# Windowed attention followed by an 8-expert mixture: GpSimd's scatters issued in smaller, more frequent turns during attention, and the first half of W2 of expert 0 staged two attention slots before the experts

## The chip, the core and the metric

The program runs on one core of a Trainium2 chip. The core has a matrix engine (TensorE, PE in the profile, with its weight loads shown as PEld), a vector engine (VectorE, DVE), a scalar engine (ScalarE, ACT), GpSimd (POOL) and SyncE (SP, which here only issues DMAs), and 16 DMA engines. The metric is the device time in microseconds of one execution; lower is better. The kernel before was timed three times.

## The reference

Two stages, all in float32. First, causal attention for 8 batches, 8 heads, 576 positions and 64 channels, with two masks: heads 0 to 3 see the last 32 positions, heads 4 to 7 every fourth of the last 128.

```python
rel = pos[:, None] - pos[None, :]
mask_plain = (rel >= 0) & (rel < window)                                   # window 32
mask_dil = (rel >= 0) & (rel < window * dilation) & (rel % dilation == 0)  # dilation 4
scores = np.where(masks[None, :, :, :], scale * q @ k.T, -1e9)
attn = softmax(scores); out = attn @ v
```

The result, as 4608 rows of 512 channels, goes through a mixture of 8 experts. Each row has noisy gate logits, the two largest pick two experts, and their softmax gives two weights:

```python
noisy_logits = x @ w_gate + np.log1p(np.exp(x @ w_noise)) * noise
top2 = np.argpartition(-noisy_logits, 2, axis=1)[:, :2]
h = np.maximum(x[mask] @ w1[e], 0.0)               # 512 -> 1024
out[mask] += top2_w[mask, k, None] * (h @ w2[e])   # 1024 -> 512
```

## The kernel before, in words

**Attention** is cut into 24 pieces (four groups of two batches, each with three pieces of dilated and three of plain heads), and runs as a software pipeline of 26 steps, each of two slots (`kb` = 2i and 2i+1). In step i the core computes the scores of piece i (`qk`, L354: mask and 24 x 4 score matmuls into the PSUM tile `s`, then on VectorE the row maximum `mx` and the shifted scores `a`), transposes the exponentials of piece i-1 (`ptr`, ScalarE copies them out as `pt`), multiplies them with the values (`pv`, output tile `x`, L426), and for piece i-2 stores `x` to DRAM (`xs`), transposes it and multiplies it with the gate matrices (`gate_mm`). `s` has one PSUM buffer and `a` one SBUF buffer; `x` has three.

**Routing** runs between these. `gate(t0, n)` (L513) is a generator for n tiles of 128 rows: some 45 small VectorE and ScalarE instructions and a few matmuls that find the two experts of each row and the slot `si` of each in a table in DRAM. Then, for each tile, one indirect DMA of GpSimd (`fill_slots`, L628) scatters the 128 entries of the first choice into the table; that of the second choice goes on `backlog`. There are 72 of these scatters. When enough of the table is there, SyncE reads it back (`ixf<-tab`), and GpSimd gathers the rows of `xs` for the first expert by 20 indirect DMAs (L770, two for each tile of 128 rows); `xsplit` transposes and splits a gathered tile.

**The order is written out by hand.** Every engine runs its instructions in the order in which the Python emits them. `micro(n)` advances the generators by n instructions (2n at rate 2). `new_slot(scatters)` is called at the end of each slot and grants GpSimd that many turns until the next grant, flushing leftovers from `backlog`; before the grant of a slot with turns is used, `pace` emits a one-element copy (`spacer<-x`) on GpSimd that reads the newest `x`, so that the turns wait for that output; the further turns of a grant are preceded by a `memset` of the spacer, which waits for nothing. Before, even slots grant 4 turns and odd slots none, and a turn of a gather takes both gathers of a tile.

**Experts.** Each expert has three blocks of rows. `up` (L814) multiplies a block with W1 in 8 column tiles `f`, three PSUM buffers in rotation, and ScalarE and VectorE turn each into `hh` and `hl`; `down` multiplies with W2 and scatters rows to the output with accumulation (L845). Work beside the matmuls is put on a schedule, `plan(t, f)`, whose clock `now` advances by the columns of the matmuls emitted (`tick`). In the first expert `some()` grants one turn every microsecond of that clock, and `some_of_slots` emits six backlog scatters in a row behind the newest `hh`. Weights pass through two staging buffers `ws` shared by W1 and W2.

Of the kernel before, what the change touches and what calls it, by code (L numbers as in the profile page):

```python
# [46 lines left out]
def attention_moe_kernel(ctx, tc, qt, kp, kd, vpl, vdl, w_gate, w_noise, noise, w1, w2, out, CAPS=(1216, 1216, 1216, 1184, 1184, 1152, 1152, 1152), SPLITS=(0, 384, 896)):  # L47
# [243 lines left out]

    fresh, backlog = [True], []

    def new_slot(scatters, speed=1):
        if scatters:
            while room[0] > 0 and backlog and not experts[0]:
                pool_turn()
                backlog.pop(0)()
            room[0], fresh[0] = scatters, True
        rate[0] = speed  # L300
        held.clear()

    def pace(yes=True):

        if yes and late["x"] is not None:
            gpsimd.tensor_copy(spacer, late["x"])  # L306
        else:
            gpsimd.memset(spacer, 0.0)

    def pool_turn():  # L310


        pace(fresh[0] and not experts[0])
        fresh[0] = False
        room[0] -= 1
# [38 lines left out]
    def qk(k):  # L354
# [22 lines left out]
        vector.tensor_tensor(a.rearrange("p y e c -> p e y c"), s[:, 0:6], mx.unsqueeze(3).to_broadcast([128, 6, 2, 64]), op=OP.subtract)  # L377
        SB[k] = a

    def expo(k):  # L380
# [379 lines left out]
    X = {}  # L760
    GT = {}

    def gather(e, t):
        r0, rn = TLS[e][t] if e != "o" else (0, 128)
        g = gp_.tile([128, 4, 128], F32, name="g")
        if e == 0:

            rows = 2304 * (next((i for i in range(U - 1) if r0 + rn <= SPLITS[i]), U - 1) + 1)
            for c in range(2):
                gpsimd.indirect_dma_start(  # L770
                    out=g[0:rn, 2 * c:2 * c + 2].rearrange("p c d -> p (c d)"), out_offset=None, in_=xs[0:rows],
                    in_offset=bass.IndirectOffsetOnAxis(ap=IX[0][0][0:rn, t, c:c + 1], axis=0))
            GT[e, t] = g
            return
        if e != "o":
            pace()
        for j in range(rn // 32):
            gpsimd.indirect_dma_start(out=g[:, j], out_offset=None, in_=xq,  # L778
                                      in_offset=bass.IndirectOffsetOnAxis(
                                          ap=IX[e][1][:, r0 // 32 + j:r0 // 32 + j + 1], axis=0))  # L780
        GT[e, t] = g
# [161 lines left out]
    def first_blocks(bi):  # L943
        for t in range(BLS[0][bi][0], BLS[0][bi][1]):
            yield from wait_turn()
            room[0] -= 1
            gather(0, t)
            if bi == 0:
# [3 lines left out]
    def split_first(bi, t):  # L952
        xsplit(0, bi, t)()
        done[bi] += 1

# [7 lines left out]

    for t0, n, kb in ((0, 9, 17), (9, 9, 29), (18, 6, 39), (24, 3, 41), (27, 6, 51)):
        at(kb, lambda t0=t0, n=n: gens.append(gate(t0, n)))
# [29 lines left out]
    for kc in range(4):  # L995
        a, b = ((-3, 2), (-2, 3), (4, 6), (5, 7))[kc]
        at(L0 + SL_W1 + a, lambda kc=kc: stage_w1(0, kc))
        at(L0 + SL_W1 + b, lambda kc=kc: late.__setitem__(("w", kc), split_w1(kc)))
        at(L0 + SL_W1 + b + 1, lambda kc=kc: late.pop(("w", kc))())
    def fillers(kb):  # L1000
        slot[0] = kb + 1
        for f in fill.pop(kb, []):
            f()
        new_slot((4, 0)[kb % 2], 1 if kb < 28 else 2)

# [72 lines left out]
    for e in range(E):  # L1078
# [12 lines left out]
        t = start if first else at_[0, 1]  # L1091
        plan(t - 6, lambda e=e: (stage_w2(EID[e], 0), stage_w2(EID[e], 1)))
        wo, ws = US_W2 if first else (0.5, 3.0)
# [4 lines left out]
        if first:  # L1098
# [22 lines left out]

            plan(start + 2.5, some_of_slots)
            plan(start + 20, lambda: gens.append(rest_of_slots()))
# [18 lines left out]
        for dn, bi, x, *ab in order:  # L1142
            if dn:
                down(x, bi, *ab)
            else:
                while e == 0 and done[bi] < BLS[0][bi][1] - BLS[0][bi][0]:
                    some()
                    tick(1200)
                up((e, bi), X.pop((e, bi)), BLS[e][bi][3], tail(e, bi))
# [84 lines left out]
```

## Time and profile before

| | |
|---|---|
| device time, median of 3 | 1091.08 us (1090.73 to 1094.09) |
| span of the profiled execution | 1086.8 us; what lies around it, against the median, is 4.3 us |
| PE / PEld busy | 1011.7 us (93%) / 855.7 us (79%) |
| DVE / ACT / POOL busy | 465.7 / 319.4 / 534.5 us |
| HBM read / written | 92.11 / 39.54 MB |
| first score matmul, first `up` matmul, first `down` matmul | 9.56, 227.24, 256.58 us |

The page gives no other time for the profiled execution than its span, so sums below are made against the span and carried to the median by the 4.3 us. A row of a timeline reads: start, duration, engine, line, operation, output<-input, shape, how many were merged, and in brackets how long the engine had been idle before and what ended that. A row of a table by windows reads: stretch, its length, then for each engine busy time and number of instructions, the granted PE clock (1.00 is full speed), the share of time the 16 DMA engines were busy, and GB/s. "remote" and "issue" stand for idle time for whose end the profile has no instruction of another engine to show.

### The profile page before, as it was taken

How to read it: one execution, taken by the hardware profiler on the slowest of the kernel's cores; microseconds unless marked ns; L12 is line 12 of the kernel's file. 1: busy time of each engine (PE TensorE's matmuls, PEld its weight loads, DVE VectorE, ACT ScalarE, POOL GpSimd, SP SyncE). 2: the span in 40 equal slices, each digit the busy share in tenths (PEclk: the TensorE clock that was granted, in tenths of full speed). 3: DMA queues.
4: the chain of work that ended last, by engine and by line, in shares of the span. 5: the costliest groups of instructions: out<-in, count | busy, mean ns of one | idle time of the engine just before them, and what ended most of it. 6: DMA issues, size and time to landing. Idle time of an engine off the chain costs nothing. (4 is left out here: it accounts for less than half of the span.)

```text
span 1086.8 us, 18768 instructions
## 1 busy us (share of the span) xinstructions
PE 1011.7 (93%) x7274; PEld 855.7 (79%) x7275; DVE 465.7 (43%) x1060; ACT 319.4 (29%) x609; POOL 534.5 (49%) x727
## 2 busy tenths in 40 slices
PE   6896877778989999999999999999999999999996
PEld 4774655567878989988997889788978888888885
DVE  7673635635225444344434352435353434343221
ACT  6673534622113322222223131312131222222110
POOL 7004243455776655755644564466455645553112
PEclk9998887878999999999999999999999999999999
DMA  8898687455255243533533352426242623453123
GB/s 280 313 315 278 194 283 257 151 164 186 43 96 129 54 109 85 109 84 86 91 85 85 86 131 50 102 64 135 38 112 52 137 39 108 75 119 72 24 28 45
DMA packets 79214, 132.95 MB, mean 122 GB/s; under 512 B 31648, under 2 KB 41296, under 8 KB 77840
## 3 DMA queue, kind: packets, MB, share of 16 engines
q1 hardware_dynamic: 56768, 92.56, 27.6%
q0 software_dynamic: 22352, 39.15, 19.6%
q8 instruction: 58, 0.95, 0.4%
q14 instruction: 36, 0.29, 0.1%
HBM read 92.11 MB, written 39.54 MB: 121 GB/s over the span
## 5 line engine op out<-in xcount | busy, mean ns | idle before, releaser
L826 PE MATMUL up<-x,w1h 128*128 128x512 f32 (+4 forms) x1536 | 396.7, 344 | 10.9 <-issue 8.2
L778 POOL DMA_INDIRECT g<-xs,ixi x258 | 269.7, 1045 | 84.0 <-issue 78.6
L826 PEld LDWEIGHTS up<-x,w1h 128*128 128x128 f32 x1536 | 273.1, 189 | 37.2 <-issue 8.7
L826 PE MATMUL up<-x,w1l 128*128 128x384 f32 (+4 forms) x768 | 263.4, 343 | 0.0
L868 PE MATMUL dn<-w2h,hh 128*128 128x512 f32 x576 | 225.5, 392 | 0.0
L868 PE MATMUL dn<-w2l,hh 128*128 128x512 f32 x576 | 224.7, 390 | 0.0
L868 PE MATMUL dn<-w2h,hl 128*128 128x512 f32 x576 | 224.6, 390 | 0.0
L832 DVE SCALAR_TENSOR_TENSOR hl<-up,hh 128x384 fp32r<-128x384 f32 (+2 forms) x192 | 106.7, 557 | 249.1 <-ACT hh L830 187.0
L830 ACT ACTIVATE hh<-up 128x384 fp32r<-128x384 f32 (+4 forms) x192 | 94.6, 498 | 298.7 <-PE up L826 248.7
L845 POOL DMA_INDIRECT out_rows<-y,ixs x67 | 107.3, 1602 | 141.4 <-DVE y L877 119.0
L826 PEld LDWEIGHTS up<-x,w1l 128*128 128x128 f32 x768 | 145.4, 189 | 11.8
L877 DVE TENSOR_SCALAR y<-dn,ixs 128x512 f32<-128x512 f32 x63 | 47.3, 751 | 188.2 <-PE dn L868 163.5
L868 PEld LDWEIGHTS dn<-w2h,hl 128*128 128x128 f32 x576 | 108.4, 188 | 22.7
L868 PEld LDWEIGHTS dn<-w2h,hh 128*128 128x128 f32 x576 | 108.5, 188 | 22.0
L868 PEld LDWEIGHTS dn<-w2l,hh 128*128 128x128 f32 x576 | 108.5, 188 | 21.8
L797 ACT CAST x<-xr 128x512 fp32r<-128x512 f32 x67 | 40.5, 605 | 216.0 <-DVE xr L795 175.8
L306 POOL COPY spacer<-hh 1x1 f32<-1x1 f32 x72 | 26.4, 366 | 131.9 <-ACT hh L830 131.6
L628 POOL DMA_INDIRECT tab<-en,si x72 | 71.8, 998 | 36.1 <-issue 16.2
L798 DVE TENSOR_TENSOR x<-xr,x 128x512 fp32r<-128x512 f32 x67 | 44.7, 667 | 17.9 <-ACT x L797 12.4
L371 PE MATMUL s<-kt,qt 128*32 128x128 f32 x1152 | 41.2, 288 | 9.9 <-DMA qt<-in_qt 5.4
L371 PEld LDWEIGHTS s<-kt,qt 128*32 128x32 f32 x1152 | 32.5, 115 | 20.3 <-issue 19.6
L708 DVE TENSOR_TENSOR w1l<-ws,w1h 128x1024 fp32r<-128x1024 f32 x32 | 38.8, 1218 | 20.8 <-ACT w1h L706 10.9
(186 smaller groups left out, 867.2 us busy)
## 6 DMA issues: line engine op xcount, KB each, us to landing
ws<-in_moe_w SPq DMA_DIRECT2D x36, 512.0 KB
ws<-in_moe_w SPq DMA_DIRECT2D x112, 128.0 KB
out_rows<-zero SPq DMA_DIRECT2D x38, 256.0 KB
vd<-in_vdl SPq DMA_DIRECT2D x24, 390.0 KB
vp<-in_vpl SPq DMA_DIRECT2D x16, 585.0 KB
qt<-in_qt SPq DMA_DIRECT2D x14, 576.0 KB
xs<-x SPq DMA_DIRECT2D x24, 256.0 KB
kt<-in_kd SPq DMA_DIRECT2D x16, 320.0 KB
```

Source lines behind the costliest of these rows:

```text
L371: tensor.matmul(s[32 * qd:32 * qd + 32, e], lhsT=QV[ty][:, b, x, 32 * ub:32 * ub + 32], rhs=KV[ty][:, :, b, x, 32 * ub:32 * ub + 64], star ...
L628: ins = gpsimd.indirect_dma_start(out=tab, out_offset=bass.IndirectOffsetOnAxis(ap=si[:, kq, t:t + 1], axis=0), in_=en[:, kq, t], in_offse ...
L708: return lambda: vector.tensor_tensor(b, s, a.bitcast(F32), op=OP.subtract)
L778: gpsimd.indirect_dma_start(out=g[:, j], out_offset=None, in_=xq, in_offset=bass.IndirectOffsetOnAxis(ap=IX[e][1][:, r0 // 32 + j:r0 // 32 ...
L797: scalar.copy(xh[:, :, o:o + rn], xr[:, :, 0:rn])
L798: return lambda: vector.tensor_tensor(xl[:, :, o:o + rn], xr[:, :, 0:rn], xh[:, :, o:o + rn].bitcast(F32), op=OP.subtract)
L826: tensor.matmul(p[:, 0:n], lhsT=a[:, 128 * f:128 * f + 128], rhs=b[:, kc, 0:n], start=(i == 0), stop=(i == 11))
L830: scalar.activation(hh[:, f, 0:n], p[:, 0:n], AF.Relu)
L832: vector.scalar_tensor_tensor(hl[:, f, 0:m], p[:, 0:m], 0.0, hh[:, f, 0:m].bitcast(F32), op0=OP.max, op1=OP.subtract)
L845: ins = gpsimd.indirect_dma_start(out=out, out_offset=bass.IndirectOffsetOnAxis(ap=sc[0:rn, t, 1:2], axis=0), in_=y[0:rn], in_offset=None, ...
L868: tensor.matmul(p[0:rn], lhsT=a[:, f, o:o + rn], rhs=b[:, f % 2], start=(i == 0), stop=(i == 23))
L877: vector.tensor_scalar(y[0:rn], p[0:rn], wsc, None, op0=OP.mult)
```

## The change

1. Slots grant 1 turn (even slots) and 2 turns (odd slots) up to slot 49, and 4 from slot 50, instead of 4 and 0. `qk` now records the shifted scores `a` as the newest tile, so the turn of an even slot waits for `a` of piece i, and the two of the odd slot for `x` of piece i-1. The tile waited for is fixed when the slot is granted (`mark`).
2. A turn takes one gather of a tile and not both; a tile is split only when both are out.
3. The first gating call of 9 tiles at slot 17 becomes one of 6 tiles at slot 15 and one of 3 at slot 17, and generators run at rate 2 from slot 16 instead of slot 28.
4. The first two quarters of W2 of expert 0 are staged in slots 49 and 50, and no longer at the first tick of the experts.
5. `some_of_slots` is planned at 10.5 instead of 2.5 us of the first expert's clock. The loop that waits for the first expert's rows no longer advances that clock.

```diff
     def new_slot(scatters, speed=1):
         if scatters:
...
-            room[0], fresh[0] = scatters, True
+            room[0], fresh[0], mark[0] = scatters, True, late["x"]
...
-    def pace(yes=True):
-
-        if yes and late["x"] is not None:
-            gpsimd.tensor_copy(spacer, late["x"])
+    def pace(yes=True, at=None):
+
+        at = late["x"] if at is None else at
+        if yes and at is not None:
+            gpsimd.tensor_copy(spacer, at)
         else:
             gpsimd.memset(spacer, 0.0)
 
     def pool_turn():
-        pace(fresh[0] and not experts[0])
+        pace(fresh[0] and not experts[0], mark[0])
...
         SB[k] = a
+        late["x"] = a[0:1, 0, 0, 0:1]
...
     def first_blocks(bi):
         for t in range(BLS[0][bi][0], BLS[0][bi][1]):
-            yield from wait_turn()
-            room[0] -= 1
-            gather(0, t)
+            for c in range(2):
+                yield from wait_turn()
+                gather(0, t, c)
...
-    for t0, n, kb in ((0, 9, 17), (9, 9, 29), (18, 6, 39), (24, 3, 41), (27, 6, 51)):
+    for t0, n, kb in ((0, 6, 15), (6, 3, 17), (9, 9, 29), (18, 6, 39), (24, 3, 41), (27, 6, 51)):
...
+    at(NK + 1, lambda: stage_w2(0, 0))
+    at(NK + 2, lambda: stage_w2(0, 1))
+
     def fillers(kb):
...
-        new_slot((4, 0)[kb % 2], 1 if kb < 28 else 2)
+        new_slot((1, 2)[kb % 2] if kb < NK + 2 else 4, 1 if kb < 16 else 2)
...
-        plan(t - 6, lambda e=e: (stage_w2(EID[e], 0), stage_w2(EID[e], 1)))
+        if not first:
+            plan(t - 6, lambda e=e: (stage_w2(EID[e], 0), stage_w2(EID[e], 1)))
...
-            plan(start + 2.5, some_of_slots)
+            plan(start + 10.5, some_of_slots)
...
                 while e == 0 and done[bi] < BLS[0][bi][1] - BLS[0][bi][0]:
                     some()
-                    tick(1200)
+                    for t in range(*BLS[0][bi][0:2]):
+                        split_first(bi, t)
```

The first place is GpSimd's order where its scatters begin, in the kernel before and then in the changed one. `tab` is the table, `en` the entries, `x` and `a` are the tiles waited for.

```order
L306 COPY spacer_172<-x_1512 1x1
L628 DMA tab_58<-en0_1452,si0_1520 37376x4
L308 MEMSET spacer_172 1x1
L628 DMA tab_58<-en0_1452,si0_1520 37376x4
L308 MEMSET spacer_172 1x1
L628 DMA tab_58<-en0_1452,si0_1520 37376x4
```

```order
L307 COPY spacer_172<-a_1366 1x1
L630 DMA tab_58<-en0_1337,si0_1406 37376x4
L307 COPY spacer_172<-x_1433 1x1
L630 DMA tab_58<-en0_1337,si0_1406 37376x4
L309 MEMSET spacer_172 1x1
L630 DMA tab_58<-en0_1337,si0_1406 37376x4
L307 COPY spacer_172<-a_1501 1x1
L630 DMA tab_58<-en0_1337,si0_1406 37376x4
```

Before, four scatters follow one wait for `x`; now one follows a wait for `a`, two a wait for the next `x`, and so on in every step, 13 times in a row (steps 11 to 23), with six gathers among these turns.

The second place is GpSimd's order in the first `up` of expert 0, before and then changed. `g<-xs` are gathers of a later block, `hh` is the tile of the `up` that the copy waits for (tile f = 0 before, f = 4 now).

```order
L770 DMA g<-xs,ixf 128x256 x2
L306 COPY spacer<-hh 1x1
L628 DMA tab<-en_2181,si_2280 37376x4
L308 MEMSET spacer 1x1
L628 DMA tab<-en_2877,si_2956 37376x4
```

```order
L773 DMA g<-xs,ixf 128x256
L307 COPY spacer<-hh 1x1
L630 DMA tab<-en_2230,si_2329 37376x4
L309 MEMSET spacer 1x1
L630 DMA tab<-en_2230,si_2329 37376x4
```

The order of the rows is the same (eight gathers stand ahead, six backlog scatters follow the copy); what the copy waits for comes four tiles later. In all, 44 scatters and 14 gathers stood ahead of this copy before; now 40 scatters and 14 gathers.

The third place is SyncE's DMA order at the end of attention, before and then changed. `ws` is the staging of W2, `xs<-x` the store of an attention output, `ixf<-tab` the table read that the gathers of the second block wait for.

```order
L988 DMA out_rows<-zero 128x512 x3
L439 DMA xs<-x 256x1x256
L441 DMA xs<-x 64x1x256 x2
L743 DMA ixf<-tab 128x4x4
L988 DMA out_rows<-zero 128x512
L712 DMA ws_3351<-in_moe_w 128x2x512
L712 DMA ws_3353<-in_moe_w 128x2x512
```

```order
L714 DMA ws_3288<-in_moe_w 128x2x512
L992 DMA out_rows<-zero 128x512
L714 DMA ws_3304<-in_moe_w 128x2x512
L441 DMA xs<-x 256x1x256
L443 DMA xs<-x 64x1x256 x2
L992 DMA out_rows<-zero 128x512 x3
L745 DMA ixf<-tab 128x4x4
```

Both W2 loads now stand ahead of the last store of `x` and of the table read; before, they stood behind both.

More of the change, by code (lines that the diff above doesn't have):

```diff
@@ L290, in attention_moe_kernel @@
     room, held, rate = [0], set(), [1]
-    fresh, backlog = [True], []
+    fresh, backlog, mark = [True], [], [None]
     def new_slot(scatters, speed=1):
@@ L760, in attention_moe_kernel, with gather @@
     X = {}
-    GT = {}
-    def gather(e, t):
+    GT, GOT = {}, {}
+    def gather(e, t, c=None):
         r0, rn = TLS[e][t] if e != "o" else (0, 128)
-        g = gp_.tile([128, 4, 128], F32, name="g")
[L766 to L774, printed above, removed]
+        if e == 0:
+            GOT[t] = c == 1
+            if c == 0:
+                GT[e, t] = gp_.tile([128, 4, 128], F32, name="g")
+            rows = 2304 * (next((i for i in range(U - 1) if r0 + rn <= SPLITS[i]), U - 1) + 1)
+            gpsimd.indirect_dma_start(
+                out=GT[e, t][0:rn, 2 * c:2 * c + 2].rearrange("p c d -> p (c d)"), out_offset=None, in_=xs[0:rows],
+                in_offset=bass.IndirectOffsetOnAxis(ap=IX[0][0][0:rn, t, c:c + 1], axis=0))
+            return
+        g = gp_.tile([128, 4, 128], F32, name="g")
         if e != "o":
@@ L952, in split_first @@
     def split_first(bi, t):
-        xsplit(0, bi, t)()
-        done[bi] += 1
+        if GOT.get(t) and (0, t) in GT:
+            xsplit(0, bi, t)()
+            done[bi] += 1
     def x_block(bi):
```

## The prediction

> **What bounds the kernel now.** I read the page first, then tables by windows, then timelines of GpSimd's bursts.
>
> ```profile
> span 1086.8 us, 18768 instructions
> PE 1011.7 (93%) x7274; PEld 855.7 (79%) x7275; DVE 465.7 (43%) x1060; ACT 319.4 (29%) x609; POOL 534.5 (49%) x727
> PEclk9998887878999999999999999999999999999999
> ```
>
> TensorE is the bound of the whole, but its clock row drops below 9 from the fourth slice to the tenth, that is up to about 270 us. The chain of waits ends in one piece at the end and says nothing on this. So I cut the span by stage:
>
> ```profile
> 53.29:77.52 24.23, 23.31 (x527) 19.05 (x521) 18.17 (x73) 17.62 (x46) 0.43 (x1) 1.00 0.93 318
> 83.44:197.62 114.18, 85.22 (x1428) 63.28 (x1426) 54.17 (x209) 49.50 (x123) 40.69 (x73) 0.82 0.75 242
> 197.62:227.24 29.62, 19.76 (x250) 14.47 (x249) 14.28 (x45) 14.61 (x35) 14.42 (x25) 0.79 0.45 137
> 227.24:256.58 29.34, 21.64 (x109) 20.86 (x108) 15.80 (x80) 7.62 (x16) 14.69 (x25) 0.75 0.63 204
> 256.58:274.98 18.40, 18.40 (x94) 15.17 (x92) 8.61 (x30) 3.17 (x6) 14.72 (x26) 1.00 0.50 154
> 256.58:1078.00 821.42, 814.60 (x4049) 701.44 (x4047) 321.10 (x534) 190.71 (x321) 442.70 (x558) 1.00 0.40 85
> ```
>
> The first stretch is four attention steps without scatters: 6.06 us each, PE busy throughout. The second is eleven steps (12 to 22): 10.4 us each. Then come the tail of attention (step 23 to the first `up`), the first `up`, the first three `down` tiles, and all from there on. From 256.58 PE is busy 814.6 of 821.4 us, though GpSimd is as dense in the fifth stretch (14.7 of 18.4 us) as in the bad ones. So GpSimd's DMAs cost TensorE nothing beside `down`, whose matmuls need few answers from other engines; whatever the change can win lies before 256.58.
>
> Which steps are slow? The scatters (L628) alone, step by step (length, busy and count, clock, DMA share, GB/s):
>
> ```profile
> 77.52:83.44 5.92, 0.00 (x0) 1.00 0.96 311
> 83.44:100.97 17.53, 7.91 (x8) 0.74 0.93 310
> 110.93:116.93 6.00, 0.00 (x0) 1.00 0.65 202
> 116.93:128.56 11.63, 3.83 (x4) 0.75 0.73 229
> 128.56:135.34 6.78, 1.95 (x2) 0.93 0.42 73
> 140.71:155.37 14.66, 7.70 (x8) 0.82 0.97 322
> 155.37:167.83 12.46, 3.84 (x4) 0.67 0.81 261
> 173.84:190.87 17.03, 1.97 (x2) 0.70 0.61 211
> ```
>
> Steps with none take 5.9 to 6.0 us, four scatters add 5.6 and 6.5 us, eight add 11.5 and 8.7, two add 0.8. (The last row has six gathers as well, so eight DMAs, and 11 us.) Gathers and scatters in the eleven steps are 32 and 6:
>
> ```profile
> 83.44:197.62 114.18, 31.05 (x32) 0.82 0.75 242
> 83.44:197.62 114.18, 5.79 (x6) 0.82 0.75 242
> ```
>
> so the excess, 114.18 - 11 x 6.0 = 48.2 us, is 1.27 us for each DMA of GpSimd, nearly its whole time in a burst. How a burst of four does it:
>
> ```profile
> 117.37 0.17 POOL L306 COPY spacer<-x 1x1 f32<-1x1 f32 x1 [11.25 <-DVE x L426]
> 118.05 0.97 POOL L628 DMA_INDIRECT tab<-en,si  x1 [0.51 <-issue]
> 121.85 0.95 POOL L628 DMA_INDIRECT tab<-en,si  x1 [0.23 <-issue]
> 123.97 0.96 DVE L376 TENSOR_REDUCE mx<-s 128x12 f32<-128x768 f32 x1 [6.01 <-remote]
> 124.08 0.86 ACT L397 COPY pt<-pp 128x512 f32<-128x512 f32 x2 [4.49 <-remote]
> 124.72 1.52 PE L414 MATMUL o<-vd,pt 128*32 128x130 f32 x20 [4.26 <-ACT pt L397]
> ```
>
> VectorE and ScalarE stand idle for 6.0 and 4.5 us, and both go on 1.2 us after the last scatter ends (122.80), with the profile naming no engine they waited for; TensorE then lacks `pt`. A burst of two at the same place:
>
> ```profile
> 130.39 0.18 POOL L306 COPY spacer<-x 1x1 f32<-1x1 f32 x1 [7.59 <-DVE x L426]
> 131.08 0.99 POOL L628 DMA_INDIRECT tab<-en,si  x1 [0.51 <-issue]
> 132.37 0.96 POOL L628 DMA_INDIRECT tab<-en,si  x1 [0.21 <-issue]
> 132.97 1.59 PE L414 MATMUL o<-vp,pt 128*32 128x130 f32 x44 [0.62 <-ACT pt L397]
> ```
>
> Here the same matmuls lose 0.62 us.
>
> **The change part by part.** *Attention turns.* Before, a grant is four DMAs behind one wait; now it is one behind `a` and two behind `x`. `a` needs VectorE to have answered TensorE (scores to `mx` to `a`) before the next DMA is issued, so no run is longer than two unless the answers have passed between. Steps 12 to 22 get 11 x 3 = 33 DMAs for 38, and step 11 gets three. The price of a pair is shown once, 0.78 us (6.78 against 6.00), 0.39 for each DMA; that of a single one behind `a` no row shows. Bounds for a step of three: nothing, since one DMA of 0.96 us fits beside ScalarE's exponential; or 3 x 1.27 = 3.8 us, as in bursts. I take the pair's row, the nearest, for all three: 1.17 us. The eleven steps then take 66.0 + 12.9 = 78.9 us and step 11 adds 1.2. A second bound is the DMA engines: the stretch moved 242 GB/s x 114.18 us = 27.6 MB, and at the 318 GB/s of the clean steps that is 87 us. Part of it is zeros for the output and W1, which no attention step waits for, so I take the middle of 78.9 and 87: 83. **Gain 114.2 - 83 - 1.2 = 30 us** (48 if spaced DMAs are free; 48.2 - 12 x 3.8 = 2.6 if each costs what it does in a burst).
>
> *Tail.* Its PE work is 19.76 us at a clock of 0.79, 15.6 us at full speed; the rest of 29.62 is stalls and low clock with 12 scatters. Now nine stand there, five of them spaced and four in a row: 15.6 + 5 x 0.39 + 4 x 1.27 = 22.6. **Gain 7 us** (0 to 14).
>
> *First `up`.* Matmul work is 21.64 us at 0.75, 16.2 at full speed. It loses its largest piece here:
>
> ```profile
> 236.95 0.95 POOL L770 DMA_INDIRECT g<-xs,ixf  x1 [0.30 <-issue]
> 237.90 0.18 POOL L306 COPY spacer<-hh 1x1 f32<-1x1 f32 x1
> 244.67 0.96 POOL L628 DMA_INDIRECT tab<-en,si  x1 [0.22 <-issue]
> 246.61 0.49 ACT L830 ACTIVATE hh<-up 128x384 fp32r<-128x384 f32 x1 [8.21 <-remote]
> 247.75 0.69 PE L826 MATMUL up<-x,w1h 128*128 128x384 f32 x1 [7.69 <-issue]
> ```
>
> Eight gathers run into six scatters, the copy between them finds its `hh` long done, ScalarE answers only when all are through, and with three PSUM buffers full TensorE waits 7.69 us. Now the copy waits for tile 4, so ScalarE must have answered five tiles before the scatters start; what is left, three tiles of `up` at 16.2 / 8 = 2.0 us and fifteen matmuls of a `down` tile at 18.40 / 72 = 0.26, together 9.9 us, covers six scatters and the 1.2 us behind them (6 x 1.27 + 1.2 = 8.8). The gathers are as dense as before, so I leave 2 us of wait and most of the low clock: 23 us. **Gain 6.5 us** (0 to 13).
>
> *W2's first half, earlier.*
>
> ```profile
> 226.31 0.96 SPq L712 DMA_DIRECT2D ws<-in_moe_w  x2
> 231.98 1.04 ACT L719 CAST w2h<-ws 128x1024 fp32r<-128x1024 f32 x1
> ```
>
> Before, it was there without a wait, 5.7 us after its issue, because `up` was slow. It is worth nothing by itself; it keeps ScalarE from standing at that cast when `up` is faster. On SyncE's queue two loads move past the last store of `x` and the table read, each waiting for a staging buffer that VectorE's W1 split frees; the gathers behind get up to 2 us later, ahead of a block that is wanted 15 us on.
>
> *Gating in two calls.* The order has 29 more VectorE rows. At no more than
>
> ```profile
> L614 DVE TENSOR_TENSOR oh<-oh,y 128x144 f32<-128x144 f32 (+2 forms) x6 | 1.5, 249 | 0.0
> ```
>
> 0.25 us each, 7 us go into steps 8 to 11, where VectorE is idle 6.1 of 24.2 us, and twice as many per place. I take 1 us of loss, up to 6 if the order puts them before `mx`.
>
> *A new wait.* `a` has one buffer, and GpSimd now reads it: VectorE's next `a` stands behind that copy, behind it the scores' only PSUM tile, and so TensorE. GpSimd is held up by
>
> ```profile
> POOL tab L628 <- DVE si L625: 15.8, 3, 10.6
> POOL g L770 <- DMA ixf<-tab: 6.2, 1, 6.2
> ```
>
> A step leaves it 6.0 - (2.94 + 1.65) = 1.4 us to spare (a pair with its copy 2.94 from the rows at 130.39, a single 1.65), so the 6.2 us wait for the table can reach TensorE with some 2 us. Loss 2 us.
>
> Sum: 30 + 7 + 6.5 - 1 - 2 = 40.5 us off the span of 1086.8, so 1046.3; with the 4.3 us between span and median, **1050.5 us**. Everything after the first `down` is taken as it is.
>
> **The rivals.** (A) *Half of it*: each spaced DMA costs about 0.9 us, or the loads of keys and values become the bound at 87 us with stalls on top. For it: clean steps already have a DMA share of 0.93 to 0.96. Against: the step from 77.52 has 0.96 and takes 5.92. Attention then wins 48.2 - 12 x 2.7 = 16 us, tail and `up` 6: 1091 - 22 + 3 = 1072.
>
> (B) *The bursts are not the cause.* Slow steps would be those whose loads are late (shares 0.93 and 0.97 in two of them); regrouping changes nothing: 1091 + 3 = 1094 with the losses, or 1091 if they are hidden. Against: steps at 0.61 and 0.73 stall as much. The page "SBUF — State Buffer" of the Trainium skill, section "Who interferes with whom", has GpSimd contend with VectorE alone, for one shared port pair, and says that PE and ACT never wait on anyone. By that rule ScalarE's 4.49 us would not be GpSimd's doing, and this rival would hold. The trace does not agree: ScalarE stood until the scatters were over.
>
> (C) *Slower*: the price goes by the DMA, and GpSimd enters the chain of every step through the single `a`. The step from 155.37 pays 6.46 / 4 = 1.6 us a scatter. At that, twelve steps of three cost 58 us against 48.2, tail and `up` stay as they are, and gating and the table wait add 3: 1091 + 10 + 3 = 1104. It decides once a DMA costs over 48.2 / 36 = 1.34 us. Against: the pair's 0.39.
>
> **How the numbers follow.** Forecast 0.62, A 0.20, B 0.07, C 0.11. The forecast alone spans 1033 (spaced DMAs free and `up` nearly clean: 48 + 8 + 5 - 3) to 1064 (0.7 us a DMA, 48 - 25, tail and `up` 7, less 3); the range for 8 in 10 reaches on through A, to 1080. A difference of 0.3%, 3.3 us, is what a measurement of this kernel can tell from none. Faster by more than that: the forecast, A, and a little of B, 0.83; within it: most of B, 0.05; slower: C and some of B, 0.12.
>
> **What would show it.** Right: attention steps from 11 on last 6 to 7.5 us each with a granted clock near 1.00; the "remote" waits of `mx` and `pt` are under 2 us; step 23 starts near 169 us and the first `up` near 191; no wait of 7.69 us in the first `up`; the part behind the first `down` keeps its 821 us. A step of 9 us or more with clean pairs, or waits of `mx` for a key or query load, would prove A; VectorE's `a` waiting for the copy of GpSimd would prove C. The sum is wrong if the stall goes by the number of DMAs and not by their runs, or if the stalls before `down` reappear as waits of `up` for the gathered rows.

## The result, and the profile after

The changed kernel took 1071.63 us at the median of four runs (1067.71 to 1075.80), the kernel before 1090.90 (1086.58 to 1094.09): a ratio of 0.983, interval 0.980 to 0.987. It is 19.3 us faster, where 40.6 was forecast. The profiled execution has these lines (span; busy time of the engines; granted clock in forty slices):

```profile
span 1066.0 us, 18824 instructions
PE 1001.5 (94%) x7275; PEld 844.3 (79%) x7276; DVE 468.1 (44%) x1088; ACT 319.8 (30%) x612; POOL 537.6 (50%) x737
PEclk9999998989899999999999999999999999999998
```

The clock row is back at 8 or more throughout. Windows of the changed kernel, cut at the same places of the program as the forecast's (step 11; steps 12 to 22; the tail; the first `up`; the first three `down` tiles; the second `up`; the second `down`; all the rest). Columns: window and length, then busy time and count of TensorE's matmuls, its weight loads, VectorE, ScalarE and GpSimd, then clock, DMA share, GB/s:

```profile
76.49:85.36 8.87, 5.84 (x131) 4.74 (x129) 4.78 (x21) 4.56 (x13) 3.52 (x6) 1.00 0.94 291
85.36:177.12 91.76, 74.55 (x1428) 56.02 (x1426) 54.27 (x213) 49.67 (x124) 34.72 (x61) 0.95 0.86 289
177.12:200.19 23.07, 17.84 (x249) 13.45 (x249) 14.34 (x44) 14.52 (x34) 13.63 (x22) 0.84 0.73 223
200.19:217.34 17.15, 17.15 (x111) 16.84 (x109) 11.78 (x63) 6.41 (x14) 9.59 (x18) 1.00 0.74 210
217.34:247.18 29.84, 23.42 (x94) 15.84 (x91) 13.35 (x54) 4.26 (x7) 21.56 (x38) 0.89 0.43 142
247.18:269.93 22.75, 22.75 (x102) 18.30 (x100) 5.59 (x8) 4.18 (x7) 14.97 (x29) 1.00 0.20 37
269.93:297.29 27.36, 21.06 (x83) 16.40 (x81) 3.81 (x6) 2.05 (x4) 20.53 (x34) 0.81 0.44 79
297.29:1066.00 768.71, 754.27 (x3777) 652.88 (x3775) 302.25 (x483) 181.61 (x304) 398.48 (x486) 1.00 0.39 83
```

The last three stages of the kernel before, which the forecast had not cut apart:

```profile
274.98:297.73 22.75, 22.75 (x102) 18.30 (x100) 5.88 (x15) 3.58 (x6) 15.79 (x26) 1.00 0.23 42
297.73:320.05 22.32, 19.59 (x84) 15.08 (x83) 4.41 (x7) 2.42 (x5) 16.41 (x26) 0.92 0.54 96
320.05:1086.80 766.75, 753.85 (x3777) 652.89 (x3775) 302.20 (x483) 181.53 (x304) 397.33 (x484) 1.00 0.39 83
```

Stage by stage, before less after: the start of step 11 comes 1.0 us earlier; step 11 loses 2.9; steps 12 to 22 gain 22.4 (114.18 to 91.76); the tail 6.6; the first `up` 12.2. The first `down` therefore starts 39.2 us earlier, at 217.34 for 256.58, and 40.5 was forecast. Then the three first `down` tiles lose 11.4 us (18.40 to 29.84), the second `down` 5.0, the rest 2.0: 18.5 us are given back where nothing was to change, and 20.8 us of the span are left.

What does the loss look like? TensorE in the second `down` (start, duration, instruction, idle time before it and what ended it), and GpSimd's DMAs there, the first and the last of 21 that follow each other with no pause of a microsecond:

```profile
278.54 0.21 PE L795 MATMUL xrp<-ident,g 64*128 64x64 f32 x1 [0.33 <-issue]
280.64 0.26 PE L795 MATMUL xrp<-ident,g 64*128 64x64 f32 x1 [1.89 <-issue]
282.77 0.26 PE L795 MATMUL xrp<-ident,g 64*128 64x64 f32 x1 [1.86 <-issue]
283.47 0.36 PE L795 MATMUL xrp<-ident,g 64*128 64x64 f32 x1 [0.44 <-issue]
285.08 0.78 PE L871 MATMUL dn<-w2h,hh 128*128 128x512 f32 x1 [1.25 <-issue]
```

```profile
254.83 0.98 POOL L630 DMA_INDIRECT tab<-en,si  x1 [4.94 <-issue]
...
281.09 1.61 POOL L848 DMA_INDIRECT out_rows<-y,ixf  x1 [0.22 <-issue]
```

Four transposes of one tile, which wait for no engine and no transfer ("issue"), start 2.10, 2.13 and 0.70 us apart: multiples of 0.70. From 277.3 to 285.2 nearly every instruction that TensorE starts, weight loads too, is 0.7 us or twice that behind the one before. It ends 2.4 us after the last DMA of the run. The same spacing fills 217.6 to 225.0, beside 14 DMAs from 208.29 on. Behind each series the granted clock is low for some microseconds more; over the two `down` windows it is 0.89 and 0.81. Until the slow starts begin, TensorE runs at full speed beside the same run of DMAs:

```profile
208.29:217.59 9.30, 9.30 (x63) 8.98 (x62) 6.19 (x27) 3.02 (x6) 7.77 (x14) 1.00 0.87 266
254.83:277.28 22.45, 22.45 (x101) 18.02 (x101) 4.84 (x7) 4.17 (x7) 18.78 (x35) 1.00 0.24 43
```

125 starts (63 matmuls and 62 weight loads) in the one, 202 in the other. From here comes the theory that the runs were to test, **S**: during an unbroken run of GpSimd's indirect DMAs each engine has a stock of starts; when it is used up, the engine starts one instruction per 0.7 us until the run is broken. Starts so spaced are called slow starts below. Its rivals: **V**, each GpSimd DMA beside `down` costs a share, however spaced; **L**, the tiles wait for late data.

**Two conditions.** The runs of this study fell into two conditions, those that ran together always into the same one: "held", where the kernel before takes 1090 to 1092 us (as in the result above; mean granted clock 0.956 to 0.973), and "free", where it takes 1027 to 1030 us (0.981 to 0.991). One chip showed both with the same program, and what sets the condition is not known. Each time below stands beside that of the kernel before in the same condition.

### The profile page after: what moved, and what is told of

Same layout as the page of the kernel before. It is cut to its first block, busy times and chain, and to the rows that moved or that the text cites. A ratio compares the mean times of both kernels' runs of the same rounds, so it can differ in the third digit from the quotient of the medians.

```text
span 1066.0 us, 18824 instructions
## 1 busy us (share of the span) xinstructions
PE 1001.5 (94%) x7275; PEld 844.3 (79%) x7276; DVE 468.1 (44%) x1088; ACT 319.8 (30%) x612; POOL 537.6 (50%) x737
## 5 line engine op out<-in xcount | busy, mean ns | idle before, releaser
L800 ACT CAST x<-xr 128x512 fp32r<-128x512 f32 x67 | 40.5, 604 | 216.6 <-DVE xr L798 173.3
L710 DVE TENSOR_TENSOR w1l<-ws,w1h 128x1024 fp32r<-128x1024 f32 x32 | 38.8, 1217 | 21.1 <-issue 11.3
L708 ACT CAST w1h<-ws 128x1024 fp32r<-128x1024 f32 x32 | 33.1, 1049 | 45.1 <-DMA ws<-in_moe_w 45.0
L798 DVE STREAM_TRANSPOSE xr<-g 128x512 f32<-128x512 f32 x67 | 45.7, 682 | 1.7 <-DMA g<-xs,ixi 1.7
```

Source lines behind the costliest of these rows:

```text
L710: return lambda: vector.tensor_tensor(b, s, a.bitcast(F32), op=OP.subtract)
L798: vector.transpose(xr[:, :, 0:rn].rearrange("p c (g t) -> p g c t", t=32), g[:, 0:n].rearrange("p g (c d) -> p g c d", d=32))
L800: scalar.copy(xh[:, :, o:o + rn], xr[:, :, 0:rn])
```

## The experiments

**Breaks in GpSimd's runs.** The edit adds ten small writes of GpSimd to its own spacer ahead of the six scatters behind the gathers, and ten in the middle of the later run:

```diff
+    def idle(n):
+        for _ in range(n):
+            gpsimd.memset(spacer, 0.0)
...
                 while backlog:
+                    if n == 8:
+                        idle(10)
                     pace(n % 4 == 0)
...
             def some_of_slots():
+                idle(10)
                 for i in range(min(6, len(backlog))):
                     pace(i == 0)
```

> The changed kernel with GpSimd idling for some 3 us (ten small writes to its spacer) at two places of the expert phase: ahead of the six table scatters that follow the eight gathers, and once in the middle of the later run of scatters and gathers. Nothing else moves. Theory S (a stock of instructions: TensorE starts some 60 to 200 instructions at full speed after GpSimd begins an unbroken run of indirect DMAs, then one each 0.7 us until the run is broken): the stalls of the first three down tiles (11.4 us) and of the second down (5.0 us) go for the most part, 1054 to 1062 us. Theory V (each GpSimd DMA beside down costs a share, however spaced): 1071 to 1078, since the same DMAs are only later. Theory L (the tiles wait for late data: gathered rows, W2's second half): 1072 to 1080, since the rows come later still.

> The kernel of the first experiment again (GpSimd idles some 3 us ahead of the six table scatters and once in the later run), for a chip with the stalls. Theory S (stock of instructions, used up in an unbroken run): from the first down to the third up 68 to 74 us instead of the changed kernel's 80; the first gather for expert 1 comes some 4 us later, which leaves 1058 to 1066. Theory V (each DMA beside down costs a share however spaced): 80 us and more, 1071 to 1078. Theory L (late data): 82 us and more, 1073 to 1080. On a chip without the stalls: 1037 to 1042, as measured.

> The kernel with two breaks of some 3 us in GpSimd's runs behind attention, once more, for a chip with the stalls. Theory S (stock of instructions, used up in an unbroken run): from the first down to the third up 68 to 74 us instead of the changed kernel's 80, 1058 to 1066. Theory V (each DMA beside down costs a share however spaced): 80 us and more, 1071 to 1078. Theory L (late data): 82 us and more, 1073 to 1080. On a chip without the stalls: 1037 to 1043, as measured twice.

Free: 1039.71 against 1027.72 (ratio 1.0125, 1.0106 to 1.0145) and 1042.22 against 1028.81 (1.012). Held, on the same chip as the second: 1068.89 against 1090.14 (0.980, 0.975 to 0.986). The writes were shorter than planned, 1.4 us, so that DMAs stand 1.7 to 2.3 us apart at a break. In the held run, the first three `down` tiles, the second `up` and the second `down`, and then the stretch from the first break to the first slow start:

```profile
226.57:256.84 30.27, 22.26 (x93) 16.89 (x91) 10.87 (x45) 3.78 (x6) 21.39 (x39) 0.83 0.32 94
256.84:279.58 22.74, 22.74 (x102) 18.30 (x100) 5.76 (x10) 4.18 (x7) 18.71 (x43) 1.00 0.23 42
279.58:297.15 17.57, 17.57 (x84) 14.24 (x82) 3.81 (x6) 2.14 (x4) 10.87 (x20) 1.00 0.51 93
```

```profile
224.43:240.94 16.51, 16.51 (x87) 13.77 (x86) 9.32 (x34) 3.47 (x7) 13.86 (x25) 1.00 0.57 208
```

The second `down` is clean: 17.57 us, TensorE busy in all of it, with nine DMAs beside it (the 27.36 us of the changed kernel have 17). That is against V. On L this run says little: the last gather for that `down` comes 2.7 us later than in the changed kernel (273.65 for 270.90), but the `down` itself begins 9.7 us later. Against L stand the four transposes of one tile above, for which the profile shows no wait for data. The first tiles lost as much as ever, but elsewhere: no slow start behind the break until 173 further starts, at 240.9, in a run that was now 20 DMAs long; then the spacing of 0.7 us until 253. S placed the stall right. From the first `down` to the third `up` it is 70.6 us, within the 68 to 74 expected. The total was missed because in this trace the first `down` came at 226.57, 9.2 us later than in the changed kernel's: 5.3 us of that were lost before the first `up` began, ahead of any break, and 4.0 us in it.

**Three breaks.** None of the runs behind attention longer than some 13 DMAs:

```diff
     def pace(yes=True, at=None):
+        if experts[0]:
+            paced[0] += 1
+            if paced[0] in (9, 19, 36):
+                for _ in range(10):
+                    gpsimd.memset(spacer, 0.0)
```

> The changed kernel with three breaks (ten small writes, 1.4 to 1.6 us) in GpSimd's runs behind attention: behind the eight gathers, ten DMAs later, and in the middle of the later run, so that none is longer than some 13 DMAs. Theory S: no stall of one instruction per 0.7 us is left before the third up; from the first down to the third up 58 to 65 us instead of 80. GpSimd's first gather for expert 1 comes at 290 to 294 us (5 later), and with 768 us behind it that now sets the end: 1058 to 1066 against 1072. Theory V (each DMA costs a share): 80 us and 1072 to 1080. Where there are no stalls: 1038 to 1045.

> The changed kernel with three breaks in GpSimd's runs behind attention, once more. Where there are stalls, theory S: from the first down to the third up 58 to 65 us instead of 80, GpSimd's first gather for expert 1 at 290 to 294 us, and 1058 to 1066 against 1072; theory V: 80 us, 1072 to 1080. Where there are none: 1039 to 1046, as measured.

Free: 1042.50 against 1028.40 (1.0146, 1.009 to 1.020). Held: 1069.11 (1066.94 to 1069.90) against 1090.24, 0.980 (0.978 to 0.981); that is not told apart from the changed kernel's 1071.63. The same three stages and the third `up`, then two waits of TensorE:

```profile
221.29:240.24 18.95, 18.66 (x93) 15.17 (x91) 11.51 (x45) 4.14 (x7) 15.40 (x40) 1.00 0.51 189
240.24:266.68 26.44, 23.18 (x102) 18.21 (x100) 6.53 (x11) 4.67 (x8) 16.84 (x31) 1.00 0.22 32
266.68:288.83 22.15, 19.54 (x82) 15.42 (x82) 3.31 (x5) 1.54 (x3) 16.30 (x37) 0.92 0.16 26
288.83:310.33 21.50, 16.32 (x97) 16.08 (x96) 5.74 (x16) 3.54 (x8) 15.51 (x23) 0.84 0.56 111
```

```profile
266.48 0.44 PE L802 MATMUL xrp<-ident,g 128*128 128x128 f32 x2 [3.26 <-DMA g<-xs,ixf]
301.21 0.87 PE L836 MATMUL up<-x,w1h 128*128 128x320 f32 x2 [5.18 <-ACT hh L840]
```

No slow start is left in these stages, and the first three tiles take 18.95 us instead of 29.84: here S holds. From the first `down` to the third `up` it is 67.5 us instead of 80.0, a little above the 58 to 65 expected. But the time hardly moves. In the place of the slow starts stand waits for GpSimd's products: rows gathered late (3.26), and a ScalarE that stands at the first rows for expert 1 while `up` wants its `hh` (5.18). Where the 12.4 us went shows beside the third `up` and the stage behind it in the changed kernel, and that stage with three breaks:

```profile
297.29:313.45 16.16, 14.55 (x97) 14.08 (x96) 6.91 (x19) 4.07 (x9) 10.51 (x13) 1.00 0.24 54
313.45:333.48 20.03, 20.03 (x90) 16.10 (x89) 11.91 (x16) 6.48 (x9) 15.02 (x18) 1.00 0.66 163
```

```profile
310.33:332.92 22.59, 20.85 (x90) 15.94 (x89) 12.05 (x19) 6.63 (x9) 16.18 (x18) 1.00 0.53 119
```

The first `down` had come 4.0 us later (221.29), the third `up` takes 5.3 us more and the next stage 2.6; the remaining 2.7 us are lost behind that.

S does not hold for every run. In the changed kernel, held, 24 DMAs (gathers for expert 1 and output scatters) follow each other from 315.60 to 350.37 us with at most 0.35 us between two, and TensorE makes 353 starts beside them, busy throughout:

```profile
315.60:350.37 34.77, 34.77 (x177) 31.17 (x176) 17.41 (x25) 9.58 (x16) 28.35 (x32) 1.00 0.55 127
```

So neither an unbroken run nor a number of starts is enough by itself; what differs there was not tested.

GpSimd's first gather for expert 1, in the changed kernel and with three breaks:

```profile
286.68 1.05 POOL L781 DMA_INDIRECT g<-xs,ixi  x1 [0.16 <-POOL spacer L307]
```

```profile
292.18 1.05 POOL L788 DMA_INDIRECT g<-xs,ixi  x1 [0.16 <-POOL spacer L314]
```

**Does GpSimd's chain set the end?** Behind that gather, 767 to 784 us pass until the end in all the traces:

| kernel | condition | that gather at, us | from it to the end of the span |
|---|---|---|---|
| before | held | 306.6 | 780.2 |
| changed | held | 286.7 | 779.4 |
| changed, two breaks / three breaks | held | 291.2 / 292.2 | 775.9 / 776.0 |
| before | free | 257.9 | 770.1 |
| changed | free | 269.0 | 767.9 |
| changed, turns undone | free | 261.1 | 768.1 |
| changed, three turns in every half-step | free | 252.3 | 775.2 |
| changed, without scatters beside `down` | free | 248.4 | 781.1 |

It is never under 767. In the free runs whose gather comes at 257.9 us or later, it is 767 to 771, which fits an end set by GpSimd; where the gather is early, or TensorE stalls, it is longer. That GpSimd sets the end is read from this floor and was not tested by itself. The changed kernel in the held condition is 12 us above the floor, so that there TensorE's path would set the end. With three breaks the gather comes 5.5 us later (2.4 us of it were there when the first `up` began), which would leave about half of the 12 to win; but that run too ends 9 us above the floor, with the losses behind the second `down` named above. No version tried here is faster than the kernel before in both conditions.

**Three turns in every half-step**, all behind `x`, to get the scatters done before the first `up` (the lines that made the single turn wait for `a` are taken out as well):

```diff
-            room[0], fresh[0], mark[0] = scatters, True, late["x"]
+            room[0], fresh[0] = scatters, True
...
-        pace(fresh[0] and not experts[0], mark[0])
+        pace(fresh[0] and not experts[0])
...
-        late["x"] = a[0:1, 0, 0, 0:1]
...
-        new_slot((1, 2)[kb % 2] if kb < NK + 2 else 4, 1 if kb < 16 else 2)
+        new_slot(3 if kb < NK + 2 else 4, 1 if kb < 16 else 2)
```

> The changed kernel with three turns in every half-step, all behind the outputs x, so that most table scatters are through before the first up. Theory G (on a chip without the stalls of 0.7 us an instruction, the end is set by GpSimd: the time from the first gather for expert 1 to the end was 767 to 771 us in seven traces, however early the first down came): some ten scatters fewer behind attention put that gather at 245 to 250 us, 1014 to 1022, below the kernel before's 1028. If TensorE's path set the end there: 1026 to 1032. On a chip with the stalls: runs of six in every step, 1095 to 1120.

> The kernel with three turns in every half-step, all behind x, once more, for a chip without the stalls. Theory G (there the end follows GpSimd: 767 to 771 us from its first gather for expert 1): that gather at 245 to 250 us, 1014 to 1022, below the kernel before's 1028. If TensorE's path set the end: 1026 to 1032. On a chip with the stalls: 1091 to 1097, as measured.

> Three turns in every half-step, all behind x. Where there are no stalls, theory G (the end follows GpSimd, 767 to 771 us from its first gather for expert 1): that gather at 245 to 250 us, 1014 to 1022, below the kernel before's 1028; if TensorE's path set the end, 1026 to 1032. Where there are stalls: 1089 to 1097, as measured twice.

Held: 1094.69 against 1091.70 (1.003, 1.001 to 1.006) and 1091.73 against 1090.14 (1.001): the gain of the change is gone, with steps of up to 16 us. Free: 1028.01 against 1028.40 (1.000). GpSimd's gather did come early, at 252.3, but attention lost 10 us in step 22, so TensorE's path set the end. The 1014 to 1022 were missed.

**The kernels themselves in the free condition.**

> The changed kernel itself, once more. The chip of the first four experiments ran the kernel before in 1027.7 us instead of 1091, and no engine there was held to one instruction per 0.7 us beside GpSimd's DMAs. On a chip without these stalls there is nothing to space: steps 12 to 22 take 66 to 68 us with the change as without it, first down some 198 us, and the time is that of the kernel before within 0.5% (1025 to 1033). On a chip that has them: 1066 to 1076 against 1086 to 1094.

> The kernel before itself, for its trace on this chip. Without the stalls: four scatters in a row leave an attention step at 6.0 to 6.5 us (1.3 to 1.7 us in all for the eleven steps, against 48.2 us in the trace that the forecast was made from), and the wait of 7.69 us in the first up is gone; 1025 to 1031. With the stalls: 1086 to 1094 and steps of 11 to 17 us.

1040.17 for the change against 1027.38 (1.0125, 1.009 to 1.016): here the change is *slower*, by 12.8 us, where I had expected no difference. The kernel before, run as an experiment, took 1029.60 (1.002). Steps 12 to 22 of the kernel before, and its first three `down` tiles:

```profile
86.05:158.05 72.00, 66.71 (x1429) 52.85 (x1426) 53.96 (x209) 49.41 (x123) 33.99 (x63) 1.00 1.00 334
206.30:225.18 18.88, 18.69 (x93) 15.17 (x92) 11.39 (x42) 3.67 (x6) 14.85 (x27) 1.00 0.62 192
```

The eleven steps, with bursts of four as ever, take 72.0 us instead of 114.18, 6.0 above eleven times 6.0 (1.3 to 1.7 had been expected), at a clock of 1.00: there is next to nothing to win by spacing. The wait of 7.69 us in the first `up` is gone. What the change costs there, in the changed kernel's trace:

```profile
157.69 1.01 POOL L773 DMA_INDIRECT g<-xs,ixf  x1 [15.37 <-DMA xs<-x]
...
159.99 0.18 POOL L307 COPY spacer<-a 1x1 f32<-1x1 f32 x1
160.20 0.96 DVE L378 TENSOR_TENSOR a<-s,mx 128x768 f32<-128x768 f32 x1 [9.01 <-POOL spacer L307]
...
161.21 0.80 PE L361 MATMUL s<-mask,identb 128*128 128x512 bf16 x2 [7.43 <-DVE a L378]
```

```profile
245.69 0.69 PE L795 MATMUL xrp<-ident,g 128*128 128x128 f32 x2 [3.86 <-DMA g<-xs,ixf]
277.94 0.87 PE L829 MATMUL up<-x,w1h 128*128 128x320 f32 x2 [5.01 <-ACT hh L833]
```

GpSimd stands 15.37 us at a gather that waits for a store of `x`; its copy from `a` stands behind that, VectorE's next `a` behind the copy for 9.01 us, and TensorE loses 7.43. The two other waits are those of a GpSimd that is late: 38 scatters were through before the first `up` instead of 44, and its gather for expert 1 comes 11 us later though the first `up` starts 5 us earlier.

**Which edit costs in the free condition?** Turns undone; the single turn moved to `x`; the single turn behind `mx`, which has two buffers; the first gating call whole:

```diff
-            room[0], fresh[0], mark[0] = scatters, True, late["x"]
+            room[0], fresh[0] = scatters, True
...
-        pace(fresh[0] and not experts[0], mark[0])
+        pace(fresh[0] and not experts[0])
...
-        late["x"] = a[0:1, 0, 0, 0:1]
...
-        new_slot((1, 2)[kb % 2] if kb < NK + 2 else 4, 1 if kb < 16 else 2)
+        new_slot((4, 0)[kb % 2], 1 if kb < 16 else 2)
```

> The changed kernel with the turns of attention alone undone: four DMAs behind one wait in every second half-step, none behind a. On a chip with the stalls of one instruction per 0.7 us: the attention steps go back to some 10 us, first down at 245 to 257 us, 1085 to 1097. On a chip without them: the 7.4 us wait of VectorE's a goes and nothing is lost, so 1026 to 1034 where the changed kernel takes 1040.

> The kernel with the turns of attention undone again, for a chip with the stalls. If the turns carry the gain up to the first down: steps 12 to 22 take 108 to 116 us again, the first down comes at 250 to 258 us, and since the scatters then stand further from down the give-back shrinks: 1085 to 1095. If the other edits carry it (the gathers in two turns, the later scatters): 1072 to 1080. On a chip without the stalls: 1026 to 1033, as measured.

1029.36 against 1028.08 (1.001, 0.999 to 1.004) and 1033.48 against 1028.81 (1.003, 1.001 to 1.006): without the turns most of the 12.8 us is gone. It never fell into the held condition, so there their worth is known from the two traces alone.

```diff
-        new_slot((1, 2)[kb % 2] if kb < NK + 2 else 4, 1 if kb < 16 else 2)
+        new_slot((0, 3)[kb % 2] if kb < NK + 2 else 4, 1 if kb < 16 else 2)
```

> The changed kernel with the three turns of a step given in one grant behind the outputs x, none behind the shifted scores a. The forecast's view (a single behind a and a pair behind x are two short runs): three in a row cost 3 x 1.27 us instead of what was measured, 3 x 0.75, so 15 to 20 us slower, 1086 to 1092. Theory S: in the changed kernel the copy of x finds x nearly done when the single ends, so they are one run of three anyway; no difference, 1068 to 1075.

1031.66 against 1027.72 (1.005, 1.003 to 1.007). Both expectations were for the held condition, so neither is tested. But without a turn behind `a` its wait is gone, and the loss is 3.9 us instead of 12.8.

```diff
-        late["x"] = a[0:1, 0, 0, 0:1]
+        late["x"] = mx[0:1, 0, 0:1]
```

> The changed kernel with the single turn behind mx, which has two buffers, instead of behind the single a. Third rival's mechanism (GpSimd enters the chain through a): on a chip without the stalls the wait of 7.43 us of TensorE for a at step 22 or 23 goes, 1031 to 1036 instead of 1040. With the stalls, where a waited for GpSimd once and for 2.0 us: 1066 to 1074, no more than 2 to 3 us better. If the wait only moves to the next thing that GpSimd holds up, no change in either.

1039.24 (1034.40 to 1044.82) against 1028.08 (1.012, 1.007 to 1.017). The profiled execution, 1032.7 us of span, has no wait for `a` beyond 2.1 us, but the median is where it was: inconclusive.

```diff
-    for t0, n, kb in ((0, 6, 15), (6, 3, 17), (9, 9, 29), (18, 6, 39), (24, 3, 41), (27, 6, 51)):
+    for t0, n, kb in ((0, 9, 17), (9, 9, 29), (18, 6, 39), (24, 3, 41), (27, 6, 51)):
...
-        new_slot((1, 2)[kb % 2] if kb < NK + 2 else 4, 1 if kb < 16 else 2)
+        new_slot((1, 2)[kb % 2] if kb < NK + 2 else 4, 1 if kb < 28 else 2)
```

> The changed kernel with the first gating call whole again (nine tiles instead of six and three) and the old rate. The forecast gave the split 1 us of loss. On a chip with the stalls: 1070 plus or minus 6, the attention's table scatters of the first gating start a step later and as many more are left for the expert phase. Without the stalls: 1036 to 1046, no difference from the changed kernel's 1040.

1038.47 against 1028.08 (1.009, 1.005 to 1.012), no difference from the change's 1.0125.

**W2 where it was.**

```diff
-    at(NK + 1, lambda: stage_w2(0, 0))
-    at(NK + 2, lambda: stage_w2(0, 1))
...
-        if not first:
-            plan(t - 6, lambda e=e: (stage_w2(EID[e], 0), stage_w2(EID[e], 1)))
+        plan(t - 6, lambda e=e: (stage_w2(EID[e], 0), stage_w2(EID[e], 1)))
```

> The changed kernel with W2's first half loaded where it was before (with the first up). The forecast gave the earlier load no worth by itself. Without the stalls: 1036 to 1044, as the changed kernel's 1040; if the first up is now too short to cover the load, the first down waits for W2 and the time is 2 to 6 us longer. With the stalls: 1068 to 1078 likewise.

Held: 1072.33 against 1091.70 (0.983, 0.980 to 0.986), the changed kernel's own ratio: the early load is worth nothing, as forecast.

**Scatters left out.** Both kernels return from the routine that issues a table scatter, in the one where the experts have begun, in the other before that:

```diff
         def fill_slots(kq, t):
+            if experts[0]:
+                return
```

> The changed kernel with the table scatters that fall into the expert phase left out (some 30 of 72; the gathers stay, and part of the table keeps its padding rows). Theories S and V: nothing dense is left on GpSimd beside down, and the 18.5 us that the changed kernel lost behind the first down come back, 1048 to 1056 us; from the first down to the end of the third up 79 us instead of 96.1. Theory L: the first three down tiles still take some 30 us, above 1064.

> The changed kernel with the table scatters that run during attention left out (those of the expert phase and all gathers stay). It measures the floor of the attention steps, which the changed kernel runs at 8.3 us each (91.8 us for steps 12 to 22). If the price is GpSimd's alone: 66 to 70 us for these eleven steps, the first down 25 to 32 us earlier, about 1042 us. If the loads of keys and values bind, as the first rival had it: 80 to 87 us, about 1062.

Both fell into the free condition: 1028.39 and 1033.87 against 1027.72 (1.000 and 1.006). The first shows what 32 scatters behind attention cost the change there, some 12 us; its gather for expert 1 comes 20.6 us earlier than the changed kernel's (248.4 for 269.0), which fits a cost through GpSimd's chain. The second could not show the price of a scatter in attention, since in this condition there is almost none.

## Why the prediction was wrong, point by point

**The step that failed** is "GpSimd's DMAs cost TensorE nothing beside `down`", and with it "Everything after the first `down` is taken as it is". It was read from one stretch of the kernel before, and that stretch had a pause of GpSimd ahead of it:

```profile
256.31 0.96 POOL L628 DMA_INDIRECT tab<-en,si  x1 [10.61 <-DVE si L625]
```

GpSimd had idled for 10.61 us when the first three tiles began. In the changed kernel eight gathers and six scatters run on without a pause from 208.29 to 226.9, 125 starts are used up in the first `up`, and the slow starts fall into `down`. With the low clock behind them they cost 11.4 us, and in the second `down`, at the end of a run of 21, 5.0. The breaks showed this (18.95 us for the three tiles, 17.57 for the second `down`). My reason, that `down` needs few answers from other engines, does not enter: even transposes without a wait were held. The kernel before had such starts too, in the second `down` at the end of a run of 18 DMAs, where the forecast did not look:

```profile
301.58 0.27 PE L792 MATMUL xrp<-ident,g 128*128 128x128 f32 x1 [0.83 <-issue]
302.99 0.32 PE L792 MATMUL xrp<-ident,g 128*128 128x128 f32 x1 [1.15 <-issue]
303.71 0.37 PE L792 MATMUL xrp<-ident,g 128*128 128x128 f32 x1 [0.39 <-issue]
```

**Steps of attention: gain 30, less 3 for gating and the wait; measured 20.5.** With 25 scatters and 6 gathers, 91.76 - 66.0 is 0.83 us for each DMA, not 0.39 (0.64 against the 72.0 us of the free run). The row that gave the 0.39, step 16 at 6.78 us, does not show the price of a pair. In the free run that leaves the scatters of attention out, the same step takes 7.66 us without any scatter (the busy time and count in this row are those of the scatters alone):

```profile
109.50:117.16 7.66, 0.00 (x0) 1.00 0.97 318
```

"No run is longer than two" did not hold either. GpSimd, and what its run held up, in step 15:

```profile
108.91 0.97 POOL L630 DMA_INDIRECT tab<-en,si  x1 [0.51 <-issue]
...
110.57 0.97 POOL L630 DMA_INDIRECT tab<-en,si  x1 [0.51 <-issue]
...
111.84 0.96 POOL L630 DMA_INDIRECT tab<-en,si  x1 [0.23 <-issue]
...
113.89 0.96 DVE L377 TENSOR_REDUCE mx<-s 128x12 f32<-128x768 f32 x1 [3.40 <-PE xtp L451]
114.00 0.86 ACT L399 COPY pt<-pp 128x512 f32<-128x512 f32 x2 [1.43 <-PE xtp L451]
```

`x` is ready when the single is through, so single and pair follow each other with 0.7 us between, less than the 1.7 us of the shortest break, and `mx` and `pt` come 1.1 and 1.2 us behind the third DMA. The forecast of steps of 6 to 7.5 us was wrong (7.6 to 8.9 us with three DMAs, up to 12.2 with six), that of a clock near 1.00 nearly right (0.95), and the "remote" waits still reached 4.1 us.

**Tail: 7; measured 6.6.** Right in size. That the spacing of the scatters did it is not shown: in the free condition, where bursts cost next to nothing, the tail shortens as well, from 29.9 us (158.05 to 187.91) to 21.9 (161.21 to 183.12).

**First `up`: 6.5; measured 12.2.** Right in sign and place, the wait of 7.69 us is gone; the size is wrong, and so is the reason. (In the held runs with W2's load where it was, with two breaks and with three this stage took 21.0, 21.1 and 18.7 us instead of 17.15; how far that comes from their edits, which fall into it, and how far from the trace is not known.) The copy that was to wait for tile 4 found it done long before, because GpSimd had stood for 6 us ahead of the gathers. By S, the run began late enough for `up` to live on its stock; what was saved there fell on `down`. **Start of the first `down`: 214 to 216 forecast, 217.34.** Right, by errors that cancel.

**W2: 0.** Right in the total (0.983 with the load where it was). **Gating split: 1 us of loss.** Not told from nothing. **The wait of the single `a`: 2 us.** In the profiled execution of the result VectorE's `a` waited for GpSimd once, 2.0 us; in the free condition TensorE lost 7.43 there. The mechanism was right, and the term depends on how late GpSimd is.

**The rivals.** A gave 1072 and the time is 1072, but not A's way: its 0.9 us a DMA is near the 0.83 measured, its tail and first `up` (6 us) were 18.7, and what it lacked was given back later; the loads do not bind at 87 us, since free runs do these steps in 72.0. B fell where the change was timed. In the free condition its premise holds, since bursts cost next to nothing there. C's mechanism, GpSimd in the chain through `a`, shows in the free runs as a wait of 7.43 us; how much of the 12.8 us it makes is not shown, since moving the single behind `mx` left the median where it was. Its price of 1.34 us a DMA was not reached.

The rule weighed in the forecast, that PE and ACT never wait on anyone (the Trainium skill, "SBUF — State Buffer", "Who interferes with whom"), stands in a section on the ports of SBUF. As a rule for every wait beside GpSimd the held runs are against it (ScalarE's `hh` "remote" for 10.9 us, TensorE's starts 0.70 us apart), while the free runs agree with it. No run shows whether a port is what the engines stood at.

## What to carry to other kernels

A stretch that is fast beside another engine's work says little before it is known what came ahead of it: look how long the other engine had been at it, and move the work in the table of the stage that receives it, too. When an engine is delayed less, follow the other engine's queue to the next point where the first one needs it (here GpSimd's first gather for the second expert); a gain ends there. Run the kernel before beside each experiment, since the same program can meet two conditions in which a change has opposite signs.

## What was not expected of the hardware

The same programs ran in two conditions: 1090 to 1092 and 1027 to 1030 us for the kernel before, 1069 to 1072 and 1040 to 1043 for the changed one and its versions with breaks. In the held one, unbroken runs of GpSimd's indirect DMAs up to 285 us left TensorE 125, 173 and 202 starts and then one per 0.70 us, and with a gap of 1.7 to 2.3 us between two DMAs the full speed came back; yet the later run of 24 DMAs left it 353 starts at full speed. In the free one, no series of slow starts is in any trace, and the eleven steps with bursts of four lose 6.0 us in all. What holds the starts is argued, not shown. That instructions arrive too late would fit. The Trainium skill, "Runtime: NRT & Kernel Launch", section "Instruction fetch mechanics", has them fetched in blocks of 16 KiB (256 instructions) ahead of use, mostly hidden. The profile's queue for them agrees in size, 58 packets and 0.95 MB for all of them, but the slow starts do not stand at the blocks' borders: the block records nearest to those from 217.6 to 225.0 are at 203.1 and 229.8 us. In the free condition gaps that fit such borders do show: single ones of 0.64 to 1.71 us before TensorE's starts number 3010, 3266, 3522, 3778 and 4034 (256 apart) in the free run with three turns in every half-step, where the DMA engines are full. What sets the condition, and whether the stock is counted in starts or in something that goes with them, stays open.
